# A gated state-space and feed-forward layer on one core: one chunk's output product as seven block products, one GELU for the last strip, later state sums

## The chip, the cores and the metric

The kernel runs on one core of a Trainium2 chip. Its five engines (TensorE or PE, VectorE or DVE, ScalarE or ACT, GpSimd or POOL, SyncE or SP) each work through a queue of their own in order and wait for one another by semaphores. The metric is the device time of one execution in microseconds. Every time here is measured on the chip.

## The reference

For x of 2048 rows and 640 columns, all in bf16, with P = 640 complex states and F = 1728 features:

```python
g = _sigmoid((x * gate_w).sum(-1, keepdims=True))
# a: a diagonal state-space layer
h = Lam_bar[None, :] * h + Bu[:, t, :]          # for each of the 2048 steps
y = 2.0 * jnp.einsum("blp,dp->bld", hseq, Cmat).real + x * Dskip[None, None, :]
# b: a feed-forward layer
h = _gelu(jnp.einsum("bsd,df->bsf", x, w1) + b1)
b = jnp.einsum("bsf,fd->bsd", h, w2) + b2
return g * a + (1 - g) * b
```

## The kernel before

The 2048 rows are cut into four chunks of 512 (`c` = 0 to 3), each of four tiles of 128 rows. Five kinds of stage follow one another on TensorE, in an order written out by hand at the end of the kernel:

- `ff1(c)`: x times w1 in 13 strips of 128 features (`kf`), 65 matmuls of 512 columns, each strip followed by one GELU on ScalarE (`ff1_act`) into `gel[c]`; a last strip of 64 features and the gate column go through `last_tile`. Strip 12 is special: its rows 0 to 95 go to block 6 of `gel[c]`, and its rows 96 to 127 by a second GELU to a tile `eL`, from which the SyncE DMA `load_e` takes them to another block. Rows 96 to 127 of block 6 hold ones, set by a GpSimd memset in `gel_tile`, so that the bias b2 comes out of the matmul.
- `ssm(c)`: x times B in 10 products of 512 columns, two for each 128 states (`ks`); ScalarE evicts each to `bu`. VectorE then turns the states, scans them along time and turns them back, in nine operations (`scan_ops`), the last of which writes a block of `hs[c]`. ScalarE turns the end of each scan into the start for the next chunk by four tiny operations (`turn_carry`, L592).
- `fin_b(c)`: gel times w2 as a 2 by 2 block product in Winograd's form, seven products of 14 matmuls of 320 columns. Its sums of blocks are made by negations on ScalarE (`minus`, L688) and adding DMAs on GpSimd's queue (`plus`, L683): `minus_c` makes N3 and `minus_d` makes N2. `fork` (L750) copies a half-made product to a second bank; `out_of` (L758) scales a finished one into `gbs`.
- `fin_a(c)`, chunk 0 only: hs times C as it stands, 80 matmuls of 320 columns. Each bank is first seeded on ScalarE with x times Dskip (`seed`, L674).
- `fin_s(c)`, chunks 1 to 3: the same product in Winograd's form, seven products of 10 matmuls. They need sums of blocks of `hs[c]` (M7, M6, M3, and g21 in place) and of C (U7, U6, U5, U4). `sum_7` makes M7 and g21 by a ScalarE negation of `hs[c]` and two adding DMAs, `sum_6` likewise M6; M3 is one VectorE addition (L847). `skip_in` adds gated x times Dskip to `gbs` on VectorE, `part_7` (L941) adds the seventh product, and `done` (L929) gives the output.

Each stage has hooks (`at`): functions called between its products, which put their instructions on the engines' queues at that point. ScalarE's and GpSimd's instructions therefore stand in the order of the calls. VectorE's are ordered by a planner with a clock for each engine (`ck`): scan operations lie in a list `pend` with a due time and a cost, `dve_now` first lets out those that are due before its own instruction, and `let_out(0, c)` lets out all that chunk c still has. Matmul results lie in eight PSUM banks (`bank`), taken in turn.

Of the kernel before, what the change touches and what calls it, by code (L numbers as in the profile page):

```python
# [16 lines left out]
P = 128  # L17
# [25 lines left out]
def kernel(  # L43
# [69 lines left out]
    eL = const.tile([P, CH], BF16, name="eL")  # L113
# [197 lines left out]
    def ff1_act(p, c, kf):  # L311
        s = kf if kf < FA else kf + 1 if kf < 2 * FA else FA
        for p0, p1 in ((0, RE), (RE, P)) if s == FA else ((0, P),):
            dst = eL[p0:p1, :] if p0 else gel[c][p0:p1, :, s, :]
            src = p[p0:p1, :] if p0 else p[p0:p1, :].rearrange("p (i t) -> p i t", i=2)
            nc.scalar.activation(out=dst, in_=src, func=ACT.Gelu_apprx_tanh, bias=b1_c[p0:p1, kf:kf + 1])  # L316
            act(0.69)
# [26 lines left out]
    def load_e(c):  # L344
        nc.sync.dma_start(out=gel[c][F_LAST:RE, :, KF - 1, :], in_=eL[RE:P, :].rearrange("p (i t) -> p i t", i=2))
# [17 lines left out]
    def gel_tile(c):  # L363
        gel[c] = gelp.tile([P, 2, KF, HT], BF16, name="gel")
        nc.gpsimd.memset(gel[c][RE:P, :, KH - 1, :], 1.0)
# [42 lines left out]
    part(1, 1)  # L408
    part(0, 3)
# [4 lines left out]
    turn_first(2, pA, pT)  # L414
# [232 lines left out]
    def gates(c):  # L647
        sl = slice(c * TPC, (c + 1) * TPC)
        engine = nc.vector if c == NCH - 1 else nc.gpsimd

        def f():
            for i, (m, b) in enumerate(((0.5, 0.5), (-0.5, 0.5), (0.5, -0.5), (-0.5, -0.5))[:4 if c > 0 else 3]):
                engine.tensor_scalar(out=gcol[:, i, sl], in0=gz[:, sl], scalar1=m, scalar2=b, op0=ALU.mult, op1=ALU.add)

        if c == NCH - 1:
            dve_now(ck.act + 0.3, 0.2, f)
        else:
            f()


    HALVES = ((0, HD), (HD, D))
    seeded = {}

    def cuts(ti):
        return ((0, HD), (HD, 512), (512, D)) if ti == NT - 1 else HALVES

    def skip(ti):
        dve_now(ck.pe, 0.4, lambda: nc.vector.tensor_tensor(out=xn[ti][:], in0=xn[ti][:], in1=Dbc[:], op=ALU.mult))

    def seed(ti):  # L670
        seeded[ti] = []
        for d0, d1 in cuts(ti):
            p = bank()
            nc.scalar.activation(out=p[:, 0:d1 - d0], in_=xn[ti][:, d0:d1], func=ACT.Identity)  # L674
            act(0.45)
            seeded[ti].append(p)
        if ti % TPC < TPC - 2:
            skip(ti + 2)
        if ti + TPC < NT - H:
            load_xn(ti + TPC)  # L680
# [43 lines left out]
    def twice(dst, src):  # L724
        plus(dst.rearrange("p (h d) -> p h d", h=2), src[:].rearrange("p (o d) -> p o d", o=1).to_broadcast([P, 2, HD]))

    def fin_b(c, at={}, gs=None):
# [54 lines left out]
        if c == NCH - 1:  # L782
            part_7()
            for j in range(H):
                twice(gs[j], gq[j])
# [5 lines left out]
        if c == NCH - 2:  # L791
            for j in range(H):
                twice(gs[j], gq[j])
# [5 lines left out]
        for j in range(0 if gs else H):  # L799
            twice(gbs[c * TPC + H + j][:], gq[j])  # L800
# [4 lines left out]

    def fin_a(c, at={}):
        let_out(0, c)
        for a in range(TPC):
            ti = c * TPC + a
            ot = fwork.tile([P, D], BF16, name="ot", bufs=4)  # L810
            if a < TPC - 2:
                seed(ti + 2)
            if a in at:
                at[a]()
            for i, (d0, d1) in enumerate(cuts(ti)):
                p = seeded[ti][i]
                for j in range(2 * KS):
                    CT = CT_re if j < KS else CT_im
                    nc.tensor.matmul(p[:, 0:d1 - d0], lhsT=hs[c][:, a // H, j // KS, j % KS, (a % H) * P:][:, 0:P], rhs=CT[:, j % KS, d0:d1],  # L819
                                     start=False, stop=(j == 2 * KS - 1), skip_group_check=True)  # L820
                    pe(d1 - d0)

                def f():
                    nc.vector.scalar_tensor_tensor(out=ot[:, d0:d1], in0=p[:, 0:d1 - d0], scalar=gcol[:, 0, ti:ti + 1],
                                                   in1=gbs[ti][:, d0:d1], op0=ALU.mult, op1=ALU.add)

                dve_now(ck.pe + 0.2, 0.45, f)
                if ti == NT - 1 and i > 0:
                    s0 = 0 if i == 1 else d0
                    q = nc.sync if i == 1 else nc.scalar  # L830
                    q.dma_start(out=out2d[ti * P:(ti + 1) * P, s0:d1], in_=ot[:, s0:d1])
            settle()
            if ti < NT - 1:
                nc.sync.dma_start(out=out2d[ti * P:(ti + 1) * P, :], in_=ot[:])
# [5 lines left out]
    def U54(c):  # L840
        return (block(N3), block(gel[1][:, 0, 0:KH, :])) if c == 1 else (block(BT_re[1]), block(BT_im[1]))

    def M3(c):
        return narrow((N2 if c == 1 else xB)[:], KS * HT).rearrange("p (k t) -> p k t", k=KS)
# [16 lines left out]
    def sum_7(c):  # L861
        let_out(0, c)
        (a, _), (g21, d) = state(c)
        minus(M7[:], g21, 1.25)
# [24 lines left out]

    def skip_in(c, tiles, d0, d1, ready=0):  # L890
# [9 lines left out]
    def fin_s(c, at={}):  # L900
        lhs, rhs = sides(c)
        spare = [narrow(gel[1][:, 1, 0:KH, :], 4 * HD)[:, j * 2 * HD:(j + 1) * 2 * HD].bitcast(F32) for j in range(H)]
# [20 lines left out]
        def done(t, j, half, h, d0=0, d1=HD):  # L923
# [5 lines left out]
            dve_now(ck.pe + 0.2, 0.47, lambda: nc.vector.scalar_tensor_tensor(  # L929
# [20 lines left out]
        for j in range(H):  # L950
            product(X, 1, j, True)
            fork(j, Y)
# [140 lines left out]
```

## Time and profile before

| what | value |
| --- | --- |
| three timed runs | 205.95 us median (205.02 to 206.21) |
| the profiled execution | 205.97 us |
| its span, first to last instruction | 204.2 us |
| PE, DVE, ACT, POOL busy | 98%, 92%, 70%, 38% of the span |
| granted TensorE clock | 1.000 |
| `ff1(2)`, `fin_a(0)`, `ssm(2)` on PE | 14.64, 10.87, 10.79 us |
| `fin_b(1)`, `fin_s(1)`, `ssm(3)` on PE | 13.50, 9.56, 10.79 us |

The profile gives start times from the beginning of the span. A row of the timeline has the start, the duration, the engine, the line of the kernel, the operation, its output and inputs by tile names, and in square brackets the idle time before it with what ended it. Operations are pipelined: two rows in succession may overlap a little, so a chain is added up by the differences of their starts.

### The profile page before, as it was taken

What the parts mean: (1) busy time and instruction counts of PE and PEld (TensorE: products, weight loads), DVE (VectorE), ACT (ScalarE), POOL (GpSimd) and SP (SyncE); (2) the same over time, 40 slices, a digit from 0 to 9 for tenths busy, and PEclk for the clock granted to TensorE, in tenths of its full rate; (3) what the DMA queues carried; (4) which work ended last, traced back from release to release, by engine and by line L of the source; (5) the groups of instructions that cost most, each with busy time, mean ns of one, the idle gap of its engine ahead of it and who ended that gap; (6) DMA issues with size and microseconds to landing.
All of it is one profiled execution on the core that took longest, in us unless ns stands there. A gap on an engine that the chain in (4) does not pass through costs nothing.

```text
span 204.2 us, 3625 instructions
## 1 busy us (share of the span) xinstructions
PE 199.4 (98%) x1291; PEld 118.7 (58%) x1291; DVE 187.9 (92%) x292; ACT 141.9 (70%) x273; POOL 77.7 (38%) x119
## 2 busy tenths in 40 slices
PE   8899999999999999999999999999999999999994
PEld 5744544444467644676446777544446777777763
DVE  2589999999999999999999999999999999999574
ACT  3498766987867898993667674297786899245620
POOL 8385399952331299032031360032150370114000
PEclk9999999999999999999999999999999999999999
DMA  7999999999699092229878998149997699819403
GB/s 185 201 142 240 201 276 164 206 231 278 113 137 239 13 166 75 64 52 205 237 131 186 235 191 130 64 104 221 289 230 148 113 204 195 176 36 207 64 0 128
DMA packets 46374, 33.06 MB, mean 162 GB/s; under 512 B 27026, under 2 KB 42804, under 8 KB 46356
## 3 DMA queue, kind: packets, MB, share of 16 engines
q0 software_dynamic: 7040, 15.05, 42.4%
q1 hardware_dynamic: 38740, 17.29, 35.4%
q10 hardware_dynamic: 576, 0.49, 0.8%
q8 instruction: 10, 0.16, 0.3%
q14 instruction: 8, 0.07, 0.1%
HBM read 7.79 MB, written 2.62 MB: 51 GB/s over the span
## 4 chain that ended last, share of the span: by engine, by line
PE 95%; DMA 2%; DVE 1%; SPq 0%; issue 0%; DVEq 0%
PE bank L307 27%; PE bank L738 26%; PE bank L481 21%; PE bank L914 14%; PE bank L819 5%; DMA xn<-in_A_x_dram 2%; PE bank L331 1%; DVE ot L929 0%; SPq L143 0%; PE bank L269 0%; DVEq L1088 0%; DVE colA L411 0%; PE bank L410 0%; PE bank L421 0%
## 5 line engine op out<-in xcount | busy, mean ns | idle before, releaser
L316 ACT ACTIVATE gel<-bank,colB 128x512 bf16<-128x512 f32 (+1 forms) x52 | 33.6, 688 | 8.2 <-PE bank L307 7.9
L573 DVE TENSOR_TENSOR_SCAN g<-r_c,carry,v 128x512 bf16<-128x512 f32 x30 | 38.5, 1284 | 0.0
L738 PEld LDWEIGHTS <-gel 128*128 128x128 bf16 x280 | 27.3, 98 | 11.1 <-issue 0.2
L484 ACT ACTIVATE bu<-bank 128x512 bf16<-128x512 f32 x40 | 22.8, 601 | 15.4 <-PE bank L481 15.3
L738 PE MATMUL bank<-w_sb,gel 128*128 128x320 bf16 x168 | 24.3, 299 | 0.0
L758 ACT ACTIVATE gb<-bank,gcol 128x320 f32<-128x320 f32 x32 | 16.1, 527 | 7.9 <-PE bank L738 7.9
L307 PEld LDWEIGHTS <-w1a_sb 128*128 128x128 bf16 x162 | 14.0, 99 | 12.0
L307 PE MATMUL bank<-xB,w1a_sb 128*128 128x512 bf16 x90 | 19.9, 380 | 0.0
L481 PE MATMUL bank<-xB,BT_re 128*128 128x512 bf16 x75 | 18.6, 380 | 0.0
L481 PE MATMUL bank<-xB,BT_im 128*128 128x512 bf16 x75 | 18.6, 379 | 0.0
L481 PEld LDWEIGHTS <-BT_im 128*128 128x128 bf16 x100 | 9.8, 98 | 11.8
L481 PEld LDWEIGHTS <-BT_re 128*128 128x128 bf16 x100 | 9.6, 98 | 11.0
L914 PEld LDWEIGHTS <-hs 128*128 128x128 bf16 x125 | 12.0, 98 | 4.5
L929 DVE SCALAR_TENSOR_TENSOR ot<-bank,gcol,gb 128x320 bf16<-128x320 f32 (+2 forms) x25 | 12.5, 535 | 1.9 <-PE bank L914 1.2
L556 DVE TENSOR_TENSOR v<-wa,bu 128x1024 bf16<-128x1024 bf16 x20 | 13.8, 688 | 0.1
L556 DVE TENSOR_TENSOR wb<-TCOS,g 128x1024 bf16<-128x1024 bf16 x20 | 13.8, 689 | 0.0
L556 DVE TENSOR_TENSOR hs<-wb,bu 128x1024 bf16<-128x1024 bf16 x20 | 13.7, 687 | 0.0
L556 DVE TENSOR_TENSOR bu<-TSIN,g 128x1024 bf16<-128x1024 bf16 x20 | 13.8, 688 | 0.0
L556 DVE TENSOR_TENSOR wa<-TCOS,bu 128x1024 bf16<-128x1024 bf16 x20 | 13.4, 672 | 0.3 <-ACT bu L484 0.3
L556 DVE TENSOR_TENSOR bu<-TSIN,bu 128x1024 bf16<-128x1024 bf16 x20 | 13.5, 676 | 0.1
L307 PE MATMUL bank<-xB,w1b_sb 128*128 128x512 bf16 x60 | 13.4, 380 | 0.0
L738 PEld LDWEIGHTS <-N 128*128 128x128 bf16 x112 | 11.0, 98 | 4.3
(201 smaller groups left out, 401.6 us busy)
## 6 DMA issues: line engine op xcount, KB each, us to landing
out_dram<-ot SPq DMA_DIRECT2D x15, 160.0 KB, 2.4
w_sb<-in_B_w_dram SPq DMA_DIRECT2D x4, 480.0 KB, 5.8
gel<-N POOLq DMA_DIRECT2D x4, 448.0 KB, 4.9
N<-gel POOLq DMA_DIRECT2D x3, 448.0 KB, 5.1
gel<-gel POOLq DMA_DIRECT2D x3, 448.0 KB, 7.6
N<-N POOLq DMA_DIRECT2D x3, 448.0 KB, 7.5
gb<-gq POOLq DMA_DIRECT2D x4, 320.0 KB, 6.7
xn<-in_A_x_dram SPq DMA_DIRECT2D x8, 160.0 KB, 5.9
```

The costliest lines, as they stand in the source:

```text
L307: nc.tensor.matmul(p[:, t0:t1], lhsT=w, rhs=xT[c][:, kd, t0:t1], start=(kd == 0) if first is None else first, stop=(kd == last), skip_grou ...
L316: nc.scalar.activation(out=dst, in_=src, func=ACT.Gelu_apprx_tanh, bias=b1_c[p0:p1, kf:kf + 1])
L331: nc.tensor.matmul(p[:, a * NL:(a + 1) * NL], lhsT=xT[c][:, kd, a * P:(a + 1) * P], rhs=w1c[kd][:, n1c - NL:n1c], start=False, stop=(kd == ...
L481: nc.tensor.matmul(p[:], lhsT=BT[ks >= KSA][:, kd, (ks % KSA if ks < KSA else ks - KSA) * P:][:, 0:P], rhs=xT[c][:, kd, :], start=(kd == 0 ...
L484: nc.scalar.activation(out=bu[:, ri, :], in_=p[:], func=ACT.Identity)
L556: nc.vector.tensor_tensor(out=o, in0=a, in1=b, op=op)
L573: nc.vector.tensor_tensor_scan(s["g"][:, ri, :], r_c[:, ks:ks + 1].to_broadcast([P, CH]), s["v"][:, ri, :], init, ALU.mult, ALU.add)
L738: nc.tensor.matmul(p[:, 0:HD], lhsT=lhs[:, s, j * P:(j + 1) * P], rhs=rhs[:, s, :], start=fresh and s == 0, stop=s == KH - 1, skip_group_c ...
L758: nc.scalar.activation(out=gbs[ti][:, h * HD:(h + 1) * HD], in_=quad[j][name][:, 0:HD], func=ACT.Identity, scale=gcol[:, 1, ti:ti + 1])
L819: nc.tensor.matmul(p[:, 0:d1 - d0], lhsT=hs[c][:, a // H, j // KS, j % KS, (a % H) * P:][:, 0:P], rhs=CT[:, j % KS, d0:d1], start=False, s ...
L914: nc.tensor.matmul(t[j][:, d0:d1], lhsT=A[i][:, k, j * P:(j + 1) * P], rhs=B[i][:, k, d0:d1], start=fresh and k == 0, stop=k == KS - 1, sk ...
L929: dve_now(ck.pe + 0.2, 0.47, lambda: nc.vector.scalar_tensor_tensor(out=ots[ti][:, o + d0:o + d1], in0=t[j][:, d0:d1], scalar=gcol[:, 0, t ...
```

## The change

Chunk 0's product with C goes through `fin_s(0)` in place of `fin_a(0)`, and the seeds are gone. Chunk 0 gets its own sums: U7, U6 and U5 on VectorE and M7, g21, U4 by DMA after `fin_b(0)`, M6 inside `ff1(2)`, M3 (in M7's tile) inside `fin_s(0)`. For chunks 0 and 2 the seventh product is scaled on ScalarE and added by doubled DMAs (`twice`); `part_7` is not used there. In chunks 2 and 3 half of `skip_in` becomes a ScalarE scaling and an adding DMA (`skip_by_dma`).

Strip 12 has one GELU for all 128 rows; `load_e` reads its rows 96 to 127 from block 6, and `ones_row` puts the ones there afterwards. `first_sums` waits for strip 12 of `ff1(1)` instead of strip 9.

Chunk 1's feature sums (`minus_c`, `minus_d`) move from `fin_a(0)` to `ssm(2)`, and its state sums a stage later: `sum_7(1)` from `ssm(2)` to the first hook of `fin_b(1)`, `sum_6(1)` from its second product to its fifth. `gates(1)` and `gates(2)` move from GpSimd to VectorE. In the start-up one transposition moves forward by one strip.

```diff
     def ff1_act(p, c, kf):
         s = kf if kf < FA else kf + 1 if kf < 2 * FA else FA
-        for p0, p1 in ((0, RE), (RE, P)) if s == FA else ((0, P),):
-            dst = eL[p0:p1, :] if p0 else gel[c][p0:p1, :, s, :]
-            src = p[p0:p1, :] if p0 else p[p0:p1, :].rearrange("p (i t) -> p i t", i=2)
-            nc.scalar.activation(out=dst, in_=src, func=ACT.Gelu_apprx_tanh, bias=b1_c[p0:p1, kf:kf + 1])
-            act(0.69)
+        nc.scalar.activation(out=gel[c][:, :, s, :], in_=p[:].rearrange("p (i t) -> p i t", i=2),
+                             func=ACT.Gelu_apprx_tanh, bias=b1_c[:, kf:kf + 1])
+        act(0.69)
...
     def load_e(c):
-        nc.sync.dma_start(out=gel[c][F_LAST:RE, :, KF - 1, :], in_=eL[RE:P, :].rearrange("p (i t) -> p i t", i=2))
+        nc.sync.dma_start(out=gel[c][F_LAST:RE, :, KF - 1, :], in_=gel[c][RE:P, :, FA, :])
+
+    def ones_row(c):
+        nc.gpsimd.memset(gel[c][RE:P, :, FA, :], 1.0)
...
     def gel_tile(c):
         gel[c] = gelp.tile([P, 2, KF, HT], BF16, name="gel")
-        nc.gpsimd.memset(gel[c][RE:P, :, KH - 1, :], 1.0)
...
     turn_first(3, pA, pT)
     part(0, 1)
     part(1, 1)
+    turn_first(2, pA, pT)
     part(0, 3)
...
-    turn_first(2, pA, pT)
     part(1, 3)
...
     def gates(c):
         sl = slice(c * TPC, (c + 1) * TPC)
-        engine = nc.vector if c == NCH - 1 else nc.gpsimd
+        engine = nc.vector if c > 0 else nc.gpsimd
 
-        if c == NCH - 1:
+        if c > 0:
             dve_now(ck.act + 0.3, 0.2, f)
         else:
             f()
...
-    def seed(ti):
-        seeded[ti] = []
-        for d0, d1 in cuts(ti):
-            p = bank()
-            nc.scalar.activation(out=p[:, 0:d1 - d0], in_=xn[ti][:, d0:d1], func=ACT.Identity)
-            act(0.45)
-            seeded[ti].append(p)
-        if ti % TPC < TPC - 2:
-            skip(ti + 2)
-        if ti + TPC < NT - H:
-            load_xn(ti + TPC)
...
-    def fin_a(c, at={}):
...
-                seed(ti + 2)
-            if a in at:
-                at[a]()
-            for i, (d0, d1) in enumerate(cuts(ti)):
-                p = seeded[ti][i]
-                for j in range(2 * KS):
-                    CT = CT_re if j < KS else CT_im
...
     def U54(c):
-        return (block(N3), block(gel[1][:, 0, 0:KH, :])) if c == 1 else (block(BT_re[1]), block(BT_im[1]))
+        return (block(N3), block(N2)) if c == 0 else (block(N3), block(gel[1][:, 0, 0:KH, :])) if c == 1 else (block(BT_re[1]), block(BT_im[1]))
 
     def M3(c):
+        if c == 0:
+            return M7[:]
...
-    def sum_7(c):
+    def sum_7(c, negate=True):
         let_out(0, c)
         (a, _), (g21, d) = state(c)
-        minus(M7[:], g21, 1.25)
+        if negate:
+            minus(M7[:], g21, 1.25)
         plus(flat(M7[:]), flat(a))
         plus(flat(g21), flat(d))
...
+    def skip_by_dma(c):
+        for a in range(H):
+            ti, g = c * TPC + a, GH[(c - 2) * H + a]
+            nc.scalar.activation(out=g, in_=xn[ti][:, 0:HD], func=ACT.Identity, scale=gcol[:, 0, ti:ti + 1])
+            act(0.42)
+            plus(gbs[ti][:, 0:HD], g)
...
+        by_dma = c in (0, 2)
...
-        for j in range(H):
-            product(X, 1, j, True)
-            fork(j, Y)
+        def first():
+            for j in range(H):
+                product(X, 1, j, True)
+                fork(j, Y)
+
+        def seventh():
+            for j in range(H):
+                product(Q, 7, j, True)
+                q[j] = spare[j] if c in (1, 2) else fwork.tile([P, HD], F32, name="gq", bufs=2)[:]
+                ti = c * TPC + H + j
+                nc.scalar.activation(out=q[j], in_=Q[j][:, 0:HD], func=ACT.Identity, scale=gcol[:, 3, ti:ti + 1] if by_dma else 1.0)
+                act(0.44)
+            for j in range(H if by_dma else 0):
+                twice(GS[c][j] if c in GS else gbs[c * TPC + H + j][:], q[j])
+
+        first()
         hook(0)
-        for j in range(H):
-            product(Q, 7, j, True)
-            q[j] = spare[j] if c == 1 else fwork.tile([P, HD], F32, name="gq", bufs=2)[:]
-            nc.scalar.activation(out=q[j], in_=Q[j][:, 0:HD], func=ACT.Identity)
-            act(0.44)
+        seventh()
         hook(1)
...
             for j in range(H):
-                skip_in(c, (H + j,), 0, D, ck.pe)
-                part_7(j)
+                if not by_dma:
+                    skip_in(c, (H + j,), 0, D, ck.pe)
+                    part_7(j)
                 product(Z, 4, j)
-                done(Z, j, 1, 0)
-            for j in range(H):
+                if not by_dma:
+                    done(Z, j, 1, 0)
+            for j in range(H):
+                if by_dma:
+                    if c > 0:
+                        skip_in(c, (H + j,), 0, D, ck.pe + 1.4)
+                    done(Z, j, 1, 0, lag=1.6)
                 done(W, j, 1, 1)
             return
...
-    ff1(1, 0, {3: lambda: (w_minus(0), w_plus(TA, B12)),
+    ff1(1, 0, {3: lambda: (w_minus(0), w_plus(TA, B12)), 4: lambda: ones_row(0),
                5: lambda: (w_minus(1), w_plus(B12, TB)),
-               9: lambda: (first_sums(), w_plus(TB, TA), w_plus(TC, TB))})
+               9: lambda: (w_plus(TB, TA), w_plus(TC, TB)),
+               12: first_sums})
+    gates(1)
     ssm(1, {2: lambda: fold(0), 4: lambda: fold(1)})
     load_xT(2)
-    fin_b(0, {1: lambda: fold(2), 2: lambda: fold(3), 3: lambda: fold(4)})
+    fin_b(0, {1: lambda: fold(2), 2: lambda: fold(3), 3: lambda: (minus(M7[:], hs[0][:, 1, 0], 1.25), fold(4))})
+    sums_76()
+    sum_7(0, False)
+    U5, U4 = U54(0)
+    dve_now(0, 0.95, lambda: nc.vector.tensor_tensor(out=U5, in0=C22, in1=U6, op=ALU.add))
     load_skip()
+    copy(U4, C21)
     gel_tile(2)
-    gates(1)
-    ff1(2, 0, {8: lambda: skips(0), 10: lambda: seed(0), 11: lambda: seed(1)})
-    fin_a(0, sums(1))
+    plus(U4, U6)
+    ones_row(1)
+    ff1(2, 0, {7: lambda: sum_6(0),
+               10: lambda: (skips(0), skips(0, H)),
+               11: lambda: skip_in(0, (H, H + 1), 0, D)})
     gates(2)
-    sums_76()
-    ssm(2, {2: lambda: sum_7(1), KS - 1: lambda: (skips(1), skips(1, H))})
+    fin_s(0, {0: lambda: skip_in(0, (0, 1), 0, D, ck.pe - 1.0), 1: lambda: (h_sums(0)[3](), [load_xn(TPC + a) for a in range(TPC)])})
+    ssm(2, {0: lambda: minus_c(1), 1: lambda: minus_d(1), KS - 1: lambda: (skips(1), skips(1, H))})
     load_xT(3)
+    ones_row(2)
     U5, U4 = U54(1)
-    fin_b(1, {1: lambda: (sum_6(1), copy(U4, C21)),
-              4: lambda: (copy(U5, C22), plus(U4, U6), plus(U5, U6)),
+    fin_b(1, {0: lambda: sum_7(1),
+              1: lambda: copy(U4, C21),
+              4: lambda: (copy(U5, C22), plus(U4, U6)),
+              2: lambda: (sum_6(1), plus(U5, U6)),
               3: lambda: skip_in(1, (0, 1), 0, HD)})
...
     fin_b(2, {1: lambda: (gated(2), sum_6(2), skips(3, H)),
-              2: lambda: (gates(3), minus_c(3)),
-              3: lambda: (gated(3), skip_in(2, (0, 1), 0, HD))}, GS[2])
-    fin_s(2, {0: lambda: (skip_in(2, (0, 1), HD, D, ck.act + 0.5), h_sums(2)[3]()), 1: lambda: (minus_d(3), skips(3))})
-    fin_b(3, {0: lambda: (let_out(1e9), [f() for f in h_sums(3)]),
-              3: lambda: skip_in(3, (0, 1), 0, HD)}, GS[3])
+              2: lambda: (gates(3), ones_row(3), skip_by_dma(2)),
+              3: lambda: minus_c(3)}, GS[2])
+    fin_s(2, {0: lambda: (h_sums(2)[3](), skip_in(2, (0, 1), HD, D, ck.act + 0.5)), 1: lambda: (minus_d(3), skips(3))})
+    fin_b(3, {0: lambda: (gated(3), let_out(1e9), [f() for f in h_sums(3)]),
+              1: lambda: skip_by_dma(3)}, GS[3])
     skip_in(3, (H, H + 1), 0, D)
     skip_in(3, (0, 1), HD, D)
     fin_s(3)
```

## The prediction

> **What bounds the kernel now.** I read the page's busy line and chain first, then the chain piece by piece, then the ScalarE (ACT) and VectorE (DVE) timelines around chunk 1, since the change moves work there.
>
> ```profile
> PE 199.4 (98%) x1291; PEld 118.7 (58%) x1291; DVE 187.9 (92%) x292; ACT 141.9 (70%) x273; POOL 77.7 (38%) x119
> ...
> PE 95%; DMA 2%; DVE 1%; SPq 0%; issue 0%; DVEq 0%
> ```
>
> The chain in order of time (start, us, what):
>
> ```profile
> 7.19 0.18 DVE colA L411
> ...
> 85.10 10.87 PE bank L819 x80
> 95.96 10.79 PE bank L481 x50
> 106.75 1.90 PE bank L738 x14
> 108.66 0.02 issue
> 108.68 11.57 PE bank L738 x84
> 120.25 9.56 PE bank L914 x70
> ```
>
> From 7.4 us to the last product TensorE (PE) sets every piece, with one hair's breadth of waiting at 108.66, in the second group of `fin_b(1)`. So an edit pays if it removes matmuls, and costs whatever it makes PE wait. ScalarE's timeline around it:
>
> ```profile
> 100.81 1.26 ACT L688 ACTIVATE M<-hs 128x1280 bf16<-128x1280 bf16 x1
> 101.97 1.10 ACT L484 ACTIVATE bu<-bank 128x512 bf16<-128x512 f32 x2
> ...
> 107.66 0.65 ACT L592 ACTIVATE carry<-g,e,cq 128x1 f32<-128x1 bf16 x2
> 108.21 0.90 ACT L750 ACTIVATE bank<-bank 128x320 f32<-128x320 f32 x2
> ```
>
> The L750 copies are the forks that the third product group of `fin_b(1)` accumulates into. They end as PE asks for them: there is no room ahead of them on ScalarE. VectorE when it ends chunk 1's states:
>
> ```profile
> 94.37 0.70 DVE L556 TENSOR_TENSOR hs<-wb,bu 128x1024 bf16<-128x1024 bf16 x1
> ...
> 96.47 0.98 DVE L875 TENSOR_TENSOR CT_re<-CT_re,CT_im 128x1600 bf16<-128x1600 bf16 x1
> 97.48 0.99 DVE L875 TENSOR_TENSOR xA<-CT_re 128x1600 bf16<-128x1600 bf16 x1
> 98.79 0.69 DVE L556 TENSOR_TENSOR wa<-TCOS,bu 128x1024 bf16<-128x1024 bf16 x1 [0.31 <-ACT bu L484]
> ```
>
> The last row of `hs[1]` is written at 94.37 to 95.07; before it VectorE is full (52.19 of the 52.40 us from 42 to 94.4 in the windows view), and only afterwards does it idle (0.31).
>
> **The parts, against the profiled execution: 205.97 us, a span of 204.2 with 1.77 around it; the median of the runs shown is 205.95, the same.**
>
> *Product.* `fin_a(0)` runs 80 matmuls in 10.87 us; `fin_s(1)` runs 70 of the same 320 columns in 9.56. Gain 1.31.
>
> *Start-up.* `turn_first(2)` leaves its place behind `colA`, where PE waits from 7.14 to 7.41 for that copy. Its tile was issued at 1.66 and takes 4.3 to land, 5.96; the new turn comes 12 matmuls after 6.13, about 6.8. Gain 0.27, down to 0 if the next transposed tiles are not in yet. I take 0.27.
>
> *GELU.* Four second passes of 0.68 go from ScalarE; PE did not wait for them: gain 0. The eight seed copies (0.42 each) give way to six forks and two evictions of 0.42 to 0.44: even. `ones_row` is the old 0.52 us POOL memset, now also waiting for `load_e`; what queues behind it on POOL, the TB sums, waits longer for TA anyway (2.16 us of idleness): 0. `first_sums` runs 3.6 us later on VectorE (45.6 to 48.8) and is first read by PE at 60.9: 0.
>
> *Sums for the new product.* U4, U5, M6 and M7 of chunk 0 have the 14.6 us of `ff1(2)`. M6's DMA leaves POOL at about 81, lands in 4.8, and is read at 88.9: 0. U4's leaves at about 78, lands in 7.6, is read at 93: 0. M3 is VectorE's: by the sum below it ends at about 91, and PE reads it at 91.7. Cost 0, bound 0.5. `skip_in` and Z's last add hang on the doubled q: issued at about 88.9, landing 6.7 (4.3 to 8.1), so in at 95.6, needed by VectorE at 97. Cost 0.
>
> *Chunk 1's state sums.* This decides. `sum_7(1)` moves from the third block of `ssm(2)` to hook 0 of `fin_b(1)`, and its negation of `hs[1]` (L688, M<-hs) now stands on ScalarE directly ahead of the two forks. Even with its input ready it puts 1.16 us (100.81 to 101.97) in front of a fork without slack. And its input is late: VectorE gets more to do before the last row of `hs[1]`. In the changed queue these stand ahead of it and did not before: U7 and U6, 2.0 (rows above); U5 of the same shape, 1.0; four wide `skip_in` of 0.88, 3.5; M3, 0.74 from start to start (125.27 to 126.01); two more output adds, 0.46 each, 0.9; four skip multiplies of chunk 1, 1.6 (105.13 to 106.74); two `gates` of 0.3, 0.6; and chunk 2's first rows woven in, four of 0.6 and a scan of 1.2, 3.6. Sum 13.9: the row starts at 94.37 + 13.9 = 108.3 and ends at 109.0. Then 1.16, a fork of 0.42 and 0.07 of handing over: PE has the fork at 110.65, and ends the stage 12 groups of 0.951 later, at 122.06. PE reaches `fin_b(1)` at 106.75 - 0.27 - 1.31 = 105.17 and asks for it 1.90 later, at 107.07. Wait 3.58; the stage already lost 0.19 there (13.50 against 13.31 in `fin_b(0)`), so +3.39. Queued behind the negation are the forks, the gate scalings that free banks, and through them every matmul. Bounds: 1.16 - 0.19 = 1.0 if VectorE is not late, about 4.5 if its new operations wait for transfers.
>
> *The sums behind it.* M7 and `hs` then leave POOL at 110, land in 5 to 6, M6 follows at 120.5 and lands at 125.4; M6 is read at 126.2, U5 (issued 121.1, 6.4) at 127.5: 0, bound 0.5. M3(1) on VectorE however waits for M6 and starts at 125.4, after idling from 123.3. In the profile 9.57 us lie between M3 (125.27) and the v row at 134.84; now a scan more (1.2) and 0.9 of waiting for PE's third product lie there: 137.1.
>
> *Chunk 2.* Before, `hs[2]` ended at 144.5 and its negation ran at 148.78 without waiting. The changed order has chunk 2 one 128-state block further behind: after 137.1 come five scans of 1.2, sixteen rows of 0.6 and two skips of 0.4, 16.4 in all, so `hs[2]` ends near 153.6. ScalarE reaches the negation between the GELUs of `ff1(3)` and holds it until then; after it, it owes 1.16 for the negation, six GELUs at 0.62, 0.31 for the bias copy, 0.4 for the last strip and 0.45 for a fork: 159.7. PE starts `ff1(3)` at 122.06 + 9.56 + 10.79 = 142.41 and asks for that fork 14.64 + 1.90 later, at 158.95. Cost 0.76; bounds 0 (no idling at 123.3) and 2.
>
> *Late chunks.* `skip_by_dma` and the doubled q of chunk 2 take about 2.8 us off VectorE (two L941 of 0.88, two of 0.5 from `skip_in`) and put six POOL DMAs on; `gated(3)` falls into ScalarE's 3.24 us of idleness at 179.15. `minus_c(3)` comes 1.9 later and its third sum queues behind two more POOL DMAs, landing near 183 against a need at 183.9 plus the shift: 0, bound 1.
>
> Sum: -1.31 - 0.27 + 3.39 + 0.76 = +2.57; 205.97 + 2.57 = 208.5.
>
> [...] The landings above come from a trace in which VectorE is full nearly throughout, and stay between 4.3 and 8.1 us for the doubled q. [...]
>
> **Rivals.**
> *The states are in time.* VectorE's lateness is the one derived number that decides. If it ends `hs[1]` by 106.9, when ScalarE has done the last eviction and the carries (107.28 to 108.21, less 1.58), only the 1.0 of the negation itself is lost, and nothing at chunk 2: 205.97 - 1.58 + 1.0 = 205.4, not slower. For it: rows of VectorE overlap a little, and the planner's costs are rough. Against: 2.1 of the 13.9 us would have to vanish, from rows measured back to back. Chance 0.13. To be faster by more than the noise, PE would also have to be rid of a wait that I do not see in the chain; all of 1.58 would be 204.4. Chance 0.06.
>
> *Transfers come late.* If POOL's new DMAs crowd each other and the doubled q takes 9.2 us, 1.1 over the longest seen, VectorE stands at Z's add until 98.1, some 0.9 after its turn; the wait passes one for one through `hs[1]` to the fork, and N2 (minus_c and minus_d now start only in `ssm(2)`, N2 landing near 109) or M6, U5 lose their margins of under 1 us: 208.5 + 0.9 + 1 = 210.4. For it: `fin_b(1)` has the DMA engines 98% busy in the windows view. Against: the late fork itself gives N2 3.5 us more. Chance 0.12.
>
> *The product does not reach 9.56.* If M3 or the first banks of `ssm(2)` are late, up to 0.5 is lost at 91.7; in the range.
>
> **How the numbers follow.** Forecast 0.69, at 208.5 with its own range 207.2 to 209.6 (start-up 0, chunk 2 from 0 to 2, VectorE half a microsecond either way). The 0.5% that a measurement of this kernel can tell is 1.03 us: faster means under 204.9, slower over 207.0. Faster 0.06; same 0.13 and 0.01 of the forecast's lower edge, 0.14; slower 0.68 + 0.12 = 0.80. The range reaches down to the case without lateness and up to the late transfers: 205.4 to 210.6.
>
> **What would show it.** `fin_s(0)` should have 70 matmuls in 9.6 us, and PE's 0.27 at 7.1 should be gone. M<-hs of chunk 1 should start on ScalarE at about 109 with VectorE's `hs` row as its releaser, and PE should show a gap of 3 to 4 us after the first 14 matmuls of `fin_b(1)`, released by the forks. A smaller gap should stand at the same place of `fin_b(2)`. No gap in `fin_b(1)`, or M<-hs starting with no wait, would make the forecast wrong; gaps in `ssm(2)` or `fin_s(1)` would make its places wrong.

## The result, and the profile after

The changed kernel is slower: 212.0 us against 205.7 on the first chip, a ratio of 1.031 (95% interval 1.025 to 1.036), and on a second chip 214.07 against 206.0, 1.037 (1.031 to 1.044). The forecast was 208.5, at most 210.6. Two of the four executions on the first chip, the profiled one among them, took 219 us at a mean granted TensorE clock of 0.984 and 0.983 (0.998 and 0.997 in the others), so the ratio is of the other two and the lines below are from a second profile of the same kernel, an execution of 214.47 us with a span of 212.6.

The page, busy line and shares of the chain:

```profile
PE 200.8 (94%) x1281; PEld 118.1 (56%) x1281; DVE 190.2 (89%) x300; ACT 142.2 (67%) x275; POOL 82.7 (39%) x124
...
PE 63%; DVE 13%; DMA 13%; ACT 4%; issue 3%; POOL 2%; SPq 0%; DVEq 0%; POOLq 0%; ACTq 0%
```

TensorE no longer sets every piece: over a third of the chain now belongs to others. Its timeline tells where (idle time and releaser in brackets):

```profile
87.54 1.52 PE L878 MATMUL bank<-CT_im,hs 128*128 128x320 bf16 x10
91.88 1.53 PE L878 MATMUL bank<-xA,M 128*128 128x320 bf16 x10 [2.82 <-DMA M<-hs]
...
112.68 2.71 PE L719 MATMUL bank<-w_sb,gel 128*128 128x320 bf16 x14 [2.40 <-ACT bank L731]
115.19 3.13 PE L719 MATMUL bank<-w_sb,N 128*128 128x320 bf16 x14
...
190.74 2.07 PE L719 MATMUL bank<-TB,N 128*128 128x320 bf16 x14 [0.36 <-DMA N<-N]
...
206.25 1.52 PE L878 MATMUL bank<-CT_im,xB 128*128 128x320 bf16 x10 [0.94 <-DVE ot L893]
```

There is a wait for M6 in `fin_s(0)` that was priced at nothing, the forecast wait for a fork in `fin_b(1)`, and two near the end. After the fork wait, 14 matmuls take 3.13 us instead of 2.06. The windows view has the cause in its PEclk column, the third number from the end (the columns are busy time by engine, granted clock, DMA share, GB/s):

```profile
112.00:114.00 2.00, 1.32 (x10) 0.97 (x10) 2.00 (x5) 1.12 (x4) 1.40 (x2) 0.99 0.99 253
114.00:116.00 2.00, 2.00 (x10) 1.08 (x9) 2.00 (x3) 0.89 (x2) 0.65 (x2) 0.50 1.05 202
116.00:118.00 2.00, 2.00 (x11) 1.26 (x10) 2.00 (x3) 0.00 (x0) 1.44 (x2) 0.66 1.07 187
```

By these rows the clock is at half rate for 3.4 us, which costs 1.7 (2.00 us times 0.01, 0.50 and 0.34). By stage on TensorE, from the starts of their first matmuls:

| stage | before | after | difference | forecast |
| --- | --- | --- | --- | --- |
| up to `fin_b(0)` | 56.98 | 56.30 | -0.68 | -0.27 |
| `fin_b(0)` | 13.32 | 13.89 | +0.57 | 0 |
| chunk 0's product | 10.87 | 12.60 | +1.73 | -1.31 |
| `fin_b(1)` | 13.50 | 17.56 | +4.06 | +3.39 |
| `fin_b(2)` | 13.32 | 13.79 | +0.47 | +0.76 |
| `fin_b(3)` | 13.31 | 14.20 | +0.89 | 0 |
| `fin_s(3)` | 9.86 | 10.79 | +0.93 | 0 |
| behind the last product | 3.03 | 3.46 | +0.43 | 0 |
| all others | | | 0 | 0 |
| sum | | | +8.40 | +2.57 |

The forecast missed by 5.83 us. Chunk 0's product has 3.04 of it and the end (`fin_b(3)` and the two rows behind it) 2.25; `fin_b(1)` is 0.67 over, a shorter wait and the half clock together, and `fin_b(0)` 0.57.

### The profile page after: what moved, and what is told of

It is laid out like the page before. It is cut to its first block, busy times and chain, and to the rows that moved or that the text cites. A ratio compares the mean times of both kernels' runs of the same rounds, so it can differ in the third digit from the quotient of the medians.

```text
span 217.1 us, 3624 instructions
## 1 busy us (share of the span) xinstructions
PE 201.8 (93%) x1270; PEld 119.1 (55%) x1281; DVE 190.4 (88%) x300; ACT 142.0 (65%) x275; POOL 82.9 (38%) x124
## 3 DMA queue, kind: packets, MB, share of 16 engines
HBM read 7.79 MB, written 2.62 MB: 48 GB/s over the span
## 5 line engine op out<-in xcount | busy, mean ns | idle before, releaser
L312 ACT ACTIVATE gel<-bank,colB 128x512 bf16<-128x512 f32 x52 | 32.8, 699 | 3.8 <-PE bank L306 3.7
L719 PE MATMUL bank<-w_sb,gel 128*128 128x320 bf16 x168 | 25.2, 305 | 3.4 <-ACT bank L731 2.7
L306 PEld LDWEIGHTS <-w1a_sb 128*128 128x128 bf16 x162 | 14.5, 101 | 12.0
L893 DVE SCALAR_TENSOR_TENSOR ot<-bank,gcol,gb 128x320 bf16<-128x320 f32 (+2 forms) x33 | 16.6, 536 | 4.6 <-PE bank L878 3.2
L878 PEld LDWEIGHTS <-hs 128*128 128x128 bf16 x165 | 16.0, 98 | 6.2
L884 ACT ACTIVATE bank<-bank 128x320 f32<-128x320 f32 (+2 forms) x23 | 9.2, 412 | 11.6 <-PE bank L878 11.5
L731 ACT ACTIVATE bank<-bank 128x320 f32<-128x320 f32 x16 | 6.6, 429 | 13.1 <-PE bank L719 13.1
L664 POOL DMA_DIRECT2D M<-hs x6 | 6.4, 1070 | 20.6 <-ACT M L669 20.6
```

Of the source, the lines that this page charges most:

```text
L306: nc.tensor.matmul(p[:, t0:t1], lhsT=w, rhs=xT[c][:, kd, t0:t1], start=(kd == 0) if first is None else first, stop=(kd == last), skip_grou ...
L312: nc.scalar.activation(out=gel[c][:, :, s, :], in_=p[:].rearrange("p (i t) -> p i t", i=2), func=ACT.Gelu_apprx_tanh, bias=b1_c[:, kf:kf + 1])
L719: nc.tensor.matmul(p[:, 0:HD], lhsT=lhs[:, s, j * P:(j + 1) * P], rhs=rhs[:, s, :], start=fresh and s == 0, stop=s == KH - 1, skip_group_c ...
L731: nc.scalar.activation(out=quad[j][dst][:, 0:HD], in_=quad[j][src][:, 0:HD], func=ACT.Identity)
L878: nc.tensor.matmul(t[j][:, d0:d1], lhsT=A[i][:, k, j * P:(j + 1) * P], rhs=B[i][:, k, d0:d1], start=fresh and k == 0, stop=k == KS - 1, sk ...
L884: nc.scalar.activation(out=dst[j][:, d0:d1], in_=X[j][:, d0:d1], func=ACT.Identity)
```

## The experiments

Each was timed beside the kernel before on the same chip; a ratio is to that kernel. *Theory* at the start: GpSimd's (POOL's) queue of adding DMAs and VectorE have no room, and the waits stand where a sum stands behind another on those two. Rivals: the clock alone; the places of the hooks alone.

**The changed kernel again.** No edit.

> The changed kernel once more, to have a profile of an execution without the half-rate clock stretches. Theory (queues): the loss of 6.2 us (205.7 to 212.0) is made by three waits of TensorE that the first profile shows, and they stand here too, whatever the clock does: about 2.6 + 0.65 us in fin_b(0) for the sums TB and TC, about 2.9 in fin_s(0) for M6, about 2.4 in fin_b(1) for the fork; with the gains of 1.3 and 0.9 this gives about 206.0 + 8.9 - 2.2 = 212.7. Rival (clock): the waits are short or absent in such an execution, under 1 us each, and matmuls that last longer than 135 ns make the loss: 206 + 6 us of stretched matmuls.

214.07 us, 1.037 (1.031 to 1.044). The waits for M6 (2.82) and the fork (2.40) are there. The wait for TB is not: `fin_b(0)` loses 0.40 to a DMA (gel<-N), where the first profile lost 2.62 + 0.65. So that part varies from execution to execution. Over all profiles of the changed kernel and its variants below, `fin_b(0)` takes 13.3 us in seven and 13.8 to 16.9 in five; what sets it is not shown. The rival is right that a half clock adds to the loss, 1.7 us here. But the clock alone is not the cause: the two executions of 212 us on the first chip had it at 0.997 and 0.998 of full speed and were still 6.3 us slower than before.

**M6's add ahead of U4's.**

```diff
-    plus(U4, U6)
-    ones_row(1)
-    ff1(2, 0, {7: lambda: sum_6(0),
+    ff1(2, 0, {7: lambda: (sum_6(0), plus(U4, U6), ones_row(1)),
```

> The changed kernel with U4's adding DMA and ones_row(1) put behind sum_6(0) on GpSimd's queue instead of ahead of it. Theory (queues): M6's add is late because it stands in order behind U4's add, which waits for U4's copy, 10.5 us in landing; free of that it leaves at 83 to 84, lands by 89, before its read at about 91.9: the 2.9 us wait in fin_s(0) goes, 212.0 to about 209.1, if nothing behind it is late. U4's add leaves as before and is in time. Rival (negation): M6 is late because ScalarE's negation waits for g21's sum; then the wait stays within 0.5 us and the time at 212. Rival (VectorE): the 2.9 us come back in fin_b(1), since VectorE's last hs row, not PE, sets the fork there: time within 0.5 us of 212, with a fork wait of 5 us in place of 2.4.

First GpSimd in the changed kernel, then in this one (N<-xA is U4's add, M<-hs is M6's):

```profile
85.48 0.89 POOL L664 DMA_DIRECT2D N<-xA  x1 [9.18 <-DVE gb L859]
...
86.51 1.22 POOL L664 DMA_DIRECT2D M<-hs  x1
```

```profile
82.70 0.89 POOL L664 DMA_DIRECT2D M<-hs  x1 [5.96 <-ACT M L669]
84.72 0.87 POOL L664 DMA_DIRECT2D N<-xA  x1 [1.14 <-PE bank L306]
```

M6's negation ended on ScalarE at 81.5 in the changed kernel, but its add left at 86.5, a memset and U4's add ahead of it; U4's add had to wait for U4's copy, issued at 75.8 and 9.1 us in landing, in at 84.9. (The releaser that the row names is the last event that the profile sees.) Turned round, M6's add leaves at 82.7, its wait is gone and `fin_s(0)` takes 10.00. The time is 212.9, 1.031 (1.024 to 1.039): 2.6 us gained in `fin_s(0)`, part of it given back, since the fork wait grew from 2.40 to 3.31. (The profiled execution, with its clock at 0.997, took 210.99; the three others, at 0.989 to 0.992, 212.7 to 213.9.) The rows of that wait:

```profile
108.50 0.68 DVE L555 TENSOR_TENSOR hs<-wb,bu 128x1024 bf16<-128x1024 bf16 x1
```

```profile
109.21 1.27 ACT L669 ACTIVATE M<-hs 128x1280 bf16<-128x1280 bf16 x1 [2.01 <-DVE hs L555]
```

```profile
110.86 1.38 PE L719 MATMUL bank<-w_sb,gel 128*128 128x320 bf16 x9 [3.31 <-ACT bank L731]
```

These are VectorE's last row of `hs[1]`, right behind it the negation on ScalarE, and TensorE with its fork. VectorE is busy for 66.03 of the 66.50 us up to that row. The forecast had the row at 108.3, the fork at 110.65 and a wait of 3.58. So theory and the VectorE rival are both right, each for its part.

**U5 three times over**, on m6_first.

```diff
-    dve_now(0, 0.95, lambda: nc.vector.tensor_tensor(out=U5, in0=C22, in1=U6, op=ALU.add))
+    for _ in range(3):
+        dve_now(0, 0.95, lambda: nc.vector.tensor_tensor(out=U5, in0=C22, in1=U6, op=ALU.add))
```

> m6_first with the sum U5 of chunk 0 made three times over on VectorE, the same result each time: 2.0 us more of VectorE work ahead of the last row of hs[1]. Theory (VectorE has no room): the fork wait in fin_b(1), 3.31 in m6_first, grows by 1.5 to 2.0 to about 5.2, and the time to 214.5. Rival (ScalarE or GpSimd late): the fork stands behind the negation and the sums of other queues, and VectorE has 1 us or more of room: the wait stays at 3.3 to 3.8 and the time within 0.5 of 212.7.

ScalarE in `fin_b(1)`:

```profile
111.34 1.27 ACT L669 ACTIVATE M<-hs 128x1280 bf16<-128x1280 bf16 x1 [5.84 <-DVE hs L555]
```

The fork wait is 6.22, 2.9 more for 2.0 us of work: the negation starts 2.1 later (the planner also put the rows in another order) and TensorE asks 0.8 earlier. The clock is at half rate for 6.8 us, 2.9 of them within the wait. 217.32 us, 1.056 (1.051 to 1.061). VectorE has no room.

**Chunk 0's skip_in left out**, on m6_first. The output of chunk 0 then lacks the term with Dskip.

```diff
-               11: lambda: skip_in(0, (H, H + 1), 0, D)})
+               })
-    fin_s(0, {0: lambda: skip_in(0, (0, 1), 0, D, ck.pe - 1.0), 1: lambda: (h_sums(0)[3](), ...
+    fin_s(0, {1: lambda: (h_sums(0)[3](), ...
```

> m6_first without skip_in(0): the four wide VectorE operations that add gated x times Dskip to chunk 0 are left out, so that chunk 0 of the output lacks that term. They take 3.34 us on VectorE in m6_first (84.11 to 85.70, 88.97 to 90.56), ahead of the last row of hs[1]. Theory (VectorE has no room): that row ends 3.2 us earlier, near 105.9, ScalarE reaches the negation at 107.2 without waiting, and the fork wait of 3.31 shrinks to about 1.1, the negation itself; with the half-rate stretches that follow a long wait gone too, 212.7 to 209.0 to 210.3, and less than 0.5 is lost in fin_b(3) and fin_s(3) where 2.0 is lost in m6_first. Rival (GpSimd's order sets the end): fin_b(3) and fin_s(3) stay at 14.3 and 10.8, since N2's add leaves as late as before; 210.3 to 211.

The fork wait fell to 0.27, further than expected. But 2.45 us are lost one stage on, in `fin_s(1)`, TensorE's timeline:

```profile
125.41 1.53 PE L878 MATMUL bank<-xA,M 128*128 128x320 bf16 x10 [1.62 <-DMA M<-hs]
127.45 1.52 PE L878 MATMUL bank<-N,hs 128*128 128x320 bf16 x10 [0.50 <-DMA N<-xA]
```

As I read it, with the sums started a stage later M6 and U5 of chunk 1 have no time left unless the fork wait itself gives it to them. `fin_b(3)` and `fin_s(3)` stay at 14.55 and 10.75: 3.3 us less on VectorE do nothing for the end, as the rival had it. 210.55 us, 1.016 (1.010 to 1.023).

**The kernel before with chunk 1's sums moved, and nothing else.**

```diff
-    fin_a(0, sums(1))
+    fin_a(0)
-    ssm(2, {2: lambda: sum_7(1), KS - 1: ...
+    ssm(2, {0: lambda: minus_c(1), 1: lambda: minus_d(1), KS - 1: ...
-    fin_b(1, {1: lambda: (sum_6(1), copy(U4, C21)),
-              4: lambda: (copy(U5, C22), plus(U4, U6), plus(U5, U6)),
+    fin_b(1, {0: lambda: sum_7(1), 1: lambda: copy(U4, C21),
+              4: lambda: (copy(U5, C22), plus(U4, U6)), 2: lambda: (sum_6(1), plus(U5, U6)),
```

> The kernel before with only chunk 1's sums moved as the change does: minus_c(1) and minus_d(1) into ssm(2), sum_7(1) to the first hook of fin_b(1), sum_6(1) to its fifth product. Chunk 0's product stays as it was, so VectorE has none of the new work and ends hs[1] near 95. Theory (VectorE's lateness, not the place, costs): only the negation itself, 1.16 us, stands ahead of the fork: wait 0.5 to 1.2, time 206.2 to 207.0. Rival (place): the fork waits 2.4 us or more here too, since N3, N2 and the state sums now crowd ScalarE and GpSimd: 208 or more.

TensorE in `fin_b(1)`:

```profile
110.05 2.06 PE L738 MATMUL bank<-w_sb,gel 128*128 128x320 bf16 x14 [1.18 <-ACT bank L750]
...
120.40 1.80 PE L738 MATMUL bank<-w_sb,gel 128*128 128x320 bf16 x12 [0.68 <-DMA gel<-N]
```

207.65 us, 1.009 (1.006 to 1.012). With VectorE in time the negation alone costs 1.18, close to the prediction's lower bound of 1.0; another 0.68 goes to the add gel<-N, which leaves as soon as TensorE has read its block (112.4) but lands in 7.9 us, 4.8 before, with the state sums' two adds just ahead of it. So about a third of the 3.31 is the place, and the rest VectorE.

**Chunk 1's state sums back in their old place**, on m6_first: `sum_7(1)` in the third block of `ssm(2)`, `sum_6(1)` in the second product of `fin_b(1)`.

> m6_first with chunk 1's state sums where the kernel before had them: sum_7(1) in the third block of ssm(2), sum_6(1) in the second product of fin_b(1). Theory (VectorE has no room, the place is not the cause): ScalarE holds the negation in ssm(2) until VectorE ends hs[1], now about 1.7 us earlier, at 107.4; six evictions stand behind it, so the fork comes at about 112.7 and TensorE waits about 5 us in place of 3.31; nothing is lost in fin_s(1); 2 to 4 us more than m6_first. Rival (the later place is the cause): the fork wait is under 1.2 us and the time 209.5 or less.

ScalarE in `ssm(2)`:

```profile
107.68 1.27 ACT L669 ACTIVATE M<-hs 128x1280 bf16<-128x1280 bf16 x1 [6.72 <-DVE hs L555]
108.86 3.02 ACT L483 ACTIVATE bu<-bank 128x512 bf16<-128x512 f32 x6
```

As the theory had it: the negation gets its row at 107.7, six evictions stand behind it, the fork wait is 5.77. 215.12 us, 1.045 (1.040 to 1.049). So the late place is not the cause: with VectorE as late, the old place waits 2.5 us longer.

**sum_7(1) behind the forks**, first alone, then with M6's add ahead (both_moves), then also with chunk 1's skip multiplications behind the last row of `hs[1]` (both_room).

```diff
-    fin_b(1, {0: lambda: sum_7(1),
-              1: lambda: copy(U4, C21),
+    fin_b(1, {1: lambda: (sum_7(1), copy(U4, C21)),
```

> The changed kernel with sum_7(1) at the second hook of fin_b(1), behind the two forks on ScalarE, instead of the first, ahead of them. Theory: the fork no longer stands behind a negation that waits for VectorE: the 2.4 us wait in fin_b(1) goes, M7 lands near 121 and is read about 1.4 us into fin_s(1), so at most 1 us comes back there: 212.0 to 209.6 (to 210.5 if M7 is late). Rival (moved on): what is late is VectorE, and the wait goes from the fork to M7, M6 or M3 in fin_s(1) in full: 211.5 to 212.5.

> The changed kernel with both repairs, M6's add ahead of U4's and sum_7(1) behind the forks. Theory (VectorE has no room): the forks are free, but the last row of hs[1] still ends near 109, so g21 lands near 118 and ScalarE holds M6's negation until then, at 115 by its turn: 1 to 2 us of the 3.31 come back in fin_s(1), in short waits that leave the clock at full rate: 210.0 to 211.0. Rival (only the place was wrong): fin_s(1) stays under 10 us and the time is 209.3 or less.

> both_moves with the four skip multiplications of chunk 1 put behind the last row of hs[1] on VectorE instead of ahead of it: 1.6 us of room for that row. Theory: what came back in fin_s(1) of both_moves shrinks by 1 to 1.6 us: 209 to 210. Rival (GpSimd or ScalarE late there): no change beyond 0.3 us against both_moves.

Alone: the fork wait is gone, and `fin_s(1)` takes 12.22 instead of 9.56, with three waits of 0.71, 0.98 and 0.50; 212.62 us, 1.032 (1.025 to 1.038). The wait moved on, nearer to the rival. With both: `fin_s(1)` 12.57, 210.52 us, 1.020 (1.015 to 1.026), as expected. With room: 210.59, 1.019 (1.015 to 1.024), no gain in the time. Its `fin_s(1)` is 11.98, 0.6 shorter where 1 to 1.6 were expected, but its profiled execution lost 1.2 in `fin_b(0)`. ScalarE of both_room shows what holds now:

```profile
119.77 1.27 ACT L669 ACTIVATE M<-hs 128x1280 bf16<-128x1280 bf16 x1 [2.72 <-DMA hs<-hs]
```

It holds M6's negation until g21's add has landed, and the evictions behind it free the banks late. The chain from M7's negation (110.65) over g21's add (left at 112.73, 7.0 in landing) and M6's negation to M6's add (left at 121.33, 3.7 in landing) takes 14.4 us, more than the 13.5 of `fin_b(1)`.

**The early edits.** early_edits is the kernel before with the start-up's move, the one GELU, `ones_row` and the later `first_sums`. early_fixed puts `ones_row(3)` ahead of the doubled q. turn_only has the start-up's move alone.

```diff
-              2: lambda: (gates(3), ones_row(3), minus_c(3)),
+    fin_b(2, {1: lambda: (gated(2), sum_6(2), skips(3, H), ones_row(3)),
+              2: lambda: (gates(3), minus_c(3)),
```

> The kernel before with only the edits ahead of ff1(2): the transposition moved in the start-up, one GELU for strip 12, ones_row, first_sums three strips later. Nothing of chunk 0's product or of the later sums. Theory (queues): ones_row(0) and the later load and sums delay TA, TB and TC on GpSimd's queue, and fin_b(0) waits 2.5 to 3.3 us for them here too; with 0.3 to 0.9 gained in the start-up the time is 207.5 to 208.8 against 205.7. Rival (as predicted): the early edits cost nothing and gain the start-up's 0.3 to 0.9: 204.8 to 205.5, and the waits for TB and TC belong to DMA traffic that differs from execution to execution.

> early_edits with ones_row(3) put at sum_6(2), ahead of the doubled q on GpSimd's queue instead of behind it. In early_edits ScalarE's N3 negation waited 1.82 us for that memset, and TensorE 1.04 for the forks behind it. Theory: that is all that the early edits cost; the time is turn_only's, 205.2 to 205.6, against 206.66. Rival: the one GELU costs in fin_b(0) too: 206 or more.

> The kernel before with only turn_first(2) moved forward in the start-up. Theory: TensorE no longer waits 0.27 us for colA, and nothing else changes: 205.6 to 205.8 against 206.0. Rival (landing): the start is set by when the tiles land, and the 0.2 to 0.7 us that the changed kernels started earlier are not the edit's: 206.0 within 0.15.

early_edits: 206.66 us, 1.004 (1.001 to 1.007). The theory falls: `fin_b(0)` takes 13.31, no wait for TB or TC. What is lost is lost in `fin_s(2)`, 1.35 us with a wait of 1.04 in it, from a place of `ones_row(3)` that the changed kernel doesn't have; ScalarE in `fin_b(2)`:

```profile
166.41 1.70 ACT L687 ACTIVATE N<-gel 128x1792 bf16<-128x1792 bf16 x1 [1.82 <-POOL gel L345]
```

It waited for the memset, which stood behind the doubled q on GpSimd. In early_fixed that is gone (`fin_s(2)` 9.61); its ratio is 0.999 (0.996 to 1.003), and turn_only's 0.999 (0.996 to 1.002). Neither can be told from the kernel before. The profiled starts of `fin_b(0)` are 56.98 and 57.20 in the two kernels without the move and 55.70 to 56.82 in the fifteen profiles with it (56.78 in turn_only). That is the forecast's direction, but the spread among the fifteen is larger than its 0.27, and before's profile also waits 0.74 for a tile of x at 5.1; the size stays open.

**The late chunks.** late_undone puts chunks 2 and 3 of m6_first back as they were (part_7 and skips on VectorE). n3_early leaves the work as the change has it, and only moves `minus_c(3)` a product forward, with `skip_by_dma(2)` behind it and the memset `ones_row(3)` ahead. both_n3 is the same step on both_moves.

```diff
     fin_b(2, {1: lambda: (gated(2), sum_6(2), skips(3, H), ones_row(3)),
-              2: lambda: (gates(3), ones_row(3), skip_by_dma(2)),
-              3: lambda: minus_c(3)}, GS[2])
+              2: lambda: (gates(3), minus_c(3)),
+              3: lambda: skip_by_dma(2)}, GS[2])
```

> m6_first with chunks 2 and 3 as in the kernel before: minus_c(3) back at the fifth hook place of fin_b(2) (ones_row(3) put ahead of it, at sum_6(2)), gated(3) back there, no skip_by_dma, and part_7 on VectorE for chunk 2. Theory (GpSimd's order): in the changed kernel N3 of chunk 3 leaves GpSimd 4.5 us later (171.7 against 167.2), so N2's sum lands at about 187.4, after its turn, and the adds behind it (gel<-N, skip_by_dma, the doubled q) are late in turn for the last outputs: fin_b(3) 14.3 in place of 13.3, fin_s(3) 10.8 in place of 9.9, the tail 0.4 more. Undone, about 2 us go: 212.7 to 210.7, and fin_b(3) is 13.3. Rival (VectorE): the end is late because VectorE is, which lags TensorE by 10.4 us at fin_b(3) in m6_first (6.5 before); then the 2.8 us of work given back to it make the end 1 to 2 us later: 213.5 to 215.

> m6_first with chunk 3's N3 sum put back a product earlier in fin_b(2) (ones_row(3) at sum_6(2), minus_c(3) at the fifth hook place, skip_by_dma(2) behind it); everything that the change took off VectorE stays off it. Theory (GpSimd's order sets the end): N3's add leaves 3 to 4 us earlier, N2's sum lands before its turn, the adds behind it follow earlier: fin_b(3) 13.3 to 13.6 in place of 14.35, fin_s(3) 10.0 to 10.4 in place of 10.78, 1.3 to 1.8 us less than m6_first. Rival (VectorE's lag sets the end): fin_s(3) stays at 10.8 or more and at most 0.7 us goes.

> both_moves with the same step as n3_early: all three repairs that leave the work as it is. Theory: both_moves less what n3_early gains on m6_first, 1.3 to 1.8: 208.5 to 209.3, still slower than before, since the 3 us in fin_s(1) that hang on VectorE stay. Rival (the waits are TensorE's slack for one another): what is gained in fin_b(3) is lost in fin_s(3), 210.0 or more.

late_undone: `fin_b(3)` is 13.31 as the theory said, but TensorE loses 1.23 + 0.56 for forks in `fin_s(2)` and 2.00 for VectorE's outputs in `fin_s(3)`: 213.69 us, 1.037 (1.031 to 1.043), the rival's sum. n3_early: `fin_s(3)` is 9.86, what it was before, but `fin_b(3)` ahead of it is 5.0 us longer than in m6_first, which gives all other engines time, so this does not tell whose wait it was. `fin_b(3)` takes 19.34, with a fork wait of 1.44, one of 2.60 and a slow stretch behind it (12 matmuls in 3.36 us, where 14 take 2.06 otherwise). VectorE there, then GpSimd:

```profile
181.05 0.55 DVE L893 SCALAR_TENSOR_TENSOR ot<-bank,gcol,gb 128x320 bf16<-128x320 f32 x1 [3.84 <-DMA gb<-BT_re]
```

```profile
171.12 0.88 POOL L664 DMA_DIRECT2D N<-gel  x1 [0.16 <-issue]
171.67 1.22 POOL L664 DMA_DIRECT2D gel<-gel  x1
172.40 2.25 POOL L664 DMA_DIRECT2D gb<-BT_re  x2
```

The skips' adds went out behind N3's two, took 8.8 us to land (5.8 in the changed kernel, where they go first), and the outputs of chunk 2 waited for them. 214.92 us, 1.043 (1.035 to 1.051); both_n3 212.67, 1.034 (1.028 to 1.039), against 210.52 for both_moves. That is over the rival's 210.0, but the other way round: `fin_s(3)` gains 0.9 and `fin_b(3)` loses 3.2. Of the two groups of adds, in both orders tried, the second is late.

The order is not all. The add that makes N2 of chunk 3 (N<-N) landed in 4.4 us in the kernel before and in 8.9 in the changed one, where chunk 2's doubled q left 4.2 us ahead of it. GpSimd in the changed kernel:

```profile
177.60 2.43 POOL L664 DMA_DIRECT2D w1a_sb<-gel  x2 [0.61 <-ACT gel L924]
181.82 0.88 POOL L664 DMA_DIRECT2D N<-N  x1 [1.79 <-PE bank L878]
191.22 0.86 POOL L664 DMA_DIRECT2D gel<-N  x1 [8.52 <-DVE hs L555]
...
194.17 2.44 POOL L664 DMA_DIRECT2D w1c_lo<-gq  x1
```

The add gel<-N takes N2 as its input and leaves 0.5 us after N2 has landed, at 190.7, whatever its row names as releaser. In n3_early N2's add leaves 4.0 us ahead of `fin_b(3)`, about as in the kernel before (4.3), and still lands in 10.5; in late_undone, without the new adds of chunk 2, it lands in 4.8. So it is the added transfers that make N2 late, more than the place in the queue.

No version beat the kernel before. The best with chunk 0's new product and all of its work are both_moves and both_room, 2% slower.

## Why the prediction was wrong

- *Product, -1.31.* Right in size: late_undone and both_room have `fin_s(0)` at 9.61.
- *Sums for the new product, 0, bound 0.5.* **This is the step that failed first.** It let M6's add leave GpSimd "at about 81" and U4's "at about 78", as if nothing stood ahead of the one and the copy that the other adds to were already in. GpSimd kept to the order of its queue: U4's add left at 85.5, after a copy that took 9.1 us, and M6's at 86.5, though its negation had ended at 81.5. Its landing, 5.3 us, was as forecast (4.8). Cost 2.82, with M3 on VectorE held by the same landing (0.84) and the skip multiplications by Dbc's (1.00).
- *Chunk 1's state sums, +3.39.* Right in mechanism and size: VectorE's last row, the negation, the fork, and the 3.58 of wait against 3.31 with M6 out of the way. In the changed kernel itself the wait is 2.40: against m6_first TensorE comes 2.7 us later and VectorE 1.8, the two waits of 1.00 and 0.84 named above. What the term lacked is the clock behind the wait, 1.7 us.
- *The sums behind it, 0, bound 0.5.* Held, but only under the fork wait's cover; no_skip_in0 shows 2.1 us there once the fork is free.
- *Chunk 2, +0.76.* Measured 0.47, a wait of 0.31 for the named fork. But ScalarE did not stand holding the negation: it came to it at 157.36, 0.16 behind the end of the last row of `hs[2]`, because its eviction at 150.53 had waited 4.88 us for VectorE. Two delays meet there, and the prediction had one of them, so that the size is near is in part luck.
- *Late chunks, 0, bound 1.* **The second step that failed**, by 2.25: the landing "near 183" of N2's sum was too early. The add left 2.3 us ahead of `fin_b(3)`, 2.0 later than before, as the 1.9 for `minus_c(3)` has it. But it took 8.9 us to land in place of 4.4, with the new adds in flight, which is 184.6 in the prediction's times. Its landing held TensorE 0.36, and the adds that had to wait for it ended with w1c_lo<-gq, landed at 201.4, when the outputs were already due: VectorE idled 0.94 for it, and TensorE 0.94 for VectorE. late_undone shows the part in `fin_b(3)`; the part in `fin_s(3)` is read from the trace alone.
- *Start-up and GELU.* The GELU's zero held (early_fixed). Of the start-up's 0.27, 0.20 stands between the profiles of turn_only and before, too little to tell from their spread.
- *The rivals.* "Transfers come late" was the nearest in kind, at 210.4, with a chance of 0.12; it looked at the doubled q and at chunk 1's N2, M6 and U5, and the late ones were chunk 0's M6 and chunk 3's N2. No run shows the 9.2 us that it assumed for chunk 0's doubled q: that landed in 6.5 in the first profile of the changed kernel, and the median of these adds from issue to landing is 6.4 there, 6.7 before. Chunk 2's take 9.3, but beside other adds in flight, and the trace doesn't tell whether those are the cause.

## What to carry to other kernels

When an operation is moved onto an in-order queue of transfers, write down for each entry when it *can* leave, the landing of its own input included, and take the running maximum down the queue: an entry that is early in need must not stand behind one that is late in input. Price each landing beside the transfers that will then be in flight, and not by its old time: here 4.4 us became 8.9. A wait that hides other chains gives them time; taking it away shows the next one, so a repair is worth the difference between the two and not the whole wait. And a wait of TensorE can cost more than itself: behind one of 2.40 us here the granted clock cost another 1.7.

## What was not expected of the hardware

Some waits of TensorE have a stretch at half the granted clock behind them, and others, as long or longer, have none. Where the windows show such a stretch while TensorE works, it is 3.4 us long or, in u5_thrice, 6.8. Within it matmuls take up to twice their time: the ten behind M6's wait took 2.85 us in the first profile of the changed kernel and 1.53 in the second. Waits of 2 us and more, and what stands behind each:

| run and stage | wait, us | behind it on TensorE |
| --- | --- | --- |
| changed kernel, first profile, `fin_b(0)` | 2.62 | full clock |
| the same, `fin_s(0)` | 2.93 | half clock for 3.4 us |
| the same, `fin_b(1)` | 2.41 | half clock for 3.4 us |
| changed kernel, second profile, `fin_s(0)` | 2.82 | full clock |
| the same, `fin_b(1)` | 2.40 | half clock for 3.4 us |
| m6_first, `fin_b(1)` | 3.31 | full clock |
| late_undone, `fin_b(1)` | 3.24 | half clock for 3.4 us |
| late_undone, `fin_s(3)` | 2.00 | 10 matmuls in 1.52 us, as otherwise |
| n3_early, `fin_b(1)` | 3.24 | 14 matmuls in 2.83 us instead of 2.06 |
| n3_early, `fin_b(3)` | 2.60 | 12 matmuls in 3.36 us |
| both_n3, `fin_b(3)` | 2.60 | 14 matmuls in 2.06 us, as otherwise |
| u5_thrice, `fin_b(1)` | 6.22 | half clock for 6.8 us, 2.9 of them within the wait |

So the length alone does not tell: 2.60 went both ways in two runs, and M6's wait in the changed kernel both ways in two executions. With no wait above 1.06, both_moves and both_room have a mean clock of 1.000 in their profiles. What decides beside the length was not shown, and that a stretch is caused by the idleness before it was read from the traces, not tried by itself.
